# Transposing keys and queries by the DMA crossbar, as 16-bit halves, in a top-k attention with a feed-forward behind it

## Chip, cores and metric

The kernel runs on one core of a Trainium2 chip, in one launch. The metric is device time in microseconds: 1582.88 us is the median of three runs (1582.7 to 1584.52). The profile that is quoted below is one execution with a span of 1580.1 us.

A core has five engines that run side by side, each working through its own instructions strictly in order: TensorE (PE, matrix products into PSUM, with its weight loads shown as PEld), VectorE (DVE), ScalarE (ACT), GpSimd (POOL) and SyncE (SP, whose queue here issues every DMA).[...] An engine whose next instruction has to wait also holds up everything behind it in its own order.

## What is computed

Attention over 8 batches of 8 heads, 576 positions and a head dimension of 64, where each query keeps only the 32 largest of its 576 scores, and then a feed-forward of 512 to 2048 to 512 with a hard-swish between, over all 4608 rows:

```python
scores = scale * np.matmul(q, k.transpose(0, 1, 3, 2))
kth = np.partition(scores, -top_k, axis=-1)[..., -top_k:-top_k + 1]
scores = np.where(scores >= kth, scores, -1e9)
attn = softmax(scores)                     # written out in the reference
x = (attn @ v) -> (B*S, H*D)
h = x @ w_in
out = (h * np.clip(h + 3, 0, 6) / 6) @ w_out
```

Everything is float32.

## The kernel before

**Pairs and duos.** Heads are taken two at a time: a `Pair` is two heads of one batch, four pairs to a batch. Its keys and queries come in as `landed` (128 partitions, nine blocks of 128 columns), and have to be transposed, so that the head dimension lies on the partitions, before TensorE can multiply them. A `Duo` is two pairs and one tile of queries, 128 rows of each of four heads; the 64 rows left over (576 = 4 x 128 + 64) make a smaller "rest" duo. Ten duos make a batch, eight full ones and two rest ones, so there are 80. The rest duos are the last two of batches 0 to 2, duos 2 and 7 of batches 3 to 6, and duos 2 and 3 of batch 7.

**The clock of the program.** The order is written out by hand (`manual_schedule`). The main loop (L562) runs over duos `m` and over eight slots `i`. In each slot VectorE does one round of the top-k search (`top`, L250 and L254: the eight largest of each row, then take them out, four rounds for each of the duo's two halves `u`). Everything else is hung on slots: the table `usual` says how many slots after its duo's start each part of a duo is issued. For half 0: `shift0` at 3, `exp0` at 4, `inverse0` at 9, `weights0` at 10, `flip0` at 12, `join0` at 15; for half 1: `shift1` 7, `exp1` 8, `inverse1` 13, `weights1` 14, `flip1` 16, `join1` 19; then `values` at 22 and `place` at 23. A slot counts as passed with the program's order, not with time, so in a rest duo, whose top-k rounds are about half as long, all the other engines get the same work in some 11 us instead of 19.4.

**A duo's way.** `scores` (PE L227 and L230, then ScalarE copies L233 and L236, in a rest duo L215 to L220) is issued in slot 1 for the next duo. `shift` runs on GpSimd (L263, L266), `exp` on ScalarE (L273, L278, with the row sums `den`, L283), `inverse` on VectorE (L287, the reciprocal of `den`), `weights` on GpSimd (L297, then L306, which splits the 32-bit weights into low and high 16-bit halves `e16`), `flip` is a DMA transpose `t16<-e16` on SP's queue (L312), `join` puts the halves together again (L318, on ScalarE for half 0, on GpSimd for half 1), and `values` multiplies by the values on PE (L338). So the weights are already transposed by the DMA crossbar, as 16-bit halves; the keys and queries are not.

**Feed-forward.** As soon as 128 rows of attention output are placed, a block of feed-forward is queued; `piece` issues it bit by bit between the slots, at a rate that `due` works out from how much is queued: h on PE (L365), evacuations on ScalarE (L373, L375), gates on GpSimd (L379, L380), the second product on PE (L385), the result on ScalarE (L395) and out by DMA (L397).

**Keys and queries.** Of the next batch, pair `p` is loaded in slot 0 of that batch's predecessor's duo 4+p (`pair_at(m, 4)`), by six DMAs, and transposed in slot 5 of duo 5+p (`pair_at(m, 5)`): `Pair.transpose` runs nine TensorE transposes into the one large PSUM tile `big` (L177), and ScalarE copies them out (L179, L180, and L183 twice, the last 64 keys of each head into `kr`). `big` has one buffer, which `scores` uses too.

**Buffers.** `kqpool` has 13 buffers of one size, which `landed`, `kq` (the transposed keys and queries), `e16`, `t16`, `eT` and, at the start, the weights `st` take in turn. In the first four duos the two feed-forward weight matrices are also converted, in 32 chunks, with work on ScalarE, GpSimd and VectorE (L102 to L123).

Of the kernel before, what the change touches and what calls it, by code (L numbers as in the profile page):

```python
# [10 lines left out]
F32 = mybir.dt.float32  # L11
U32 = mybir.dt.uint32
I32 = mybir.dt.int32
U16 = mybir.dt.uint16
# [15 lines left out]
def kernel(  # L30
# [9 lines left out]
    nc = tc.nc  # L40
    P = nc.NUM_PARTITIONS
    B, H, S, D = q.shape
    DM, FF = moe_w_in.shape
    J = S // P
    JP = J * P
    R = S - JP
# [6 lines left out]
    def pool(name, bufs, **kw):  # L53
        return ctx.enter_context(tc.tile_pool(name=name, bufs=bufs, **kw))

    consts = pool("consts", 1)
    kqpool = pool("kq", 13)
    scpool = pool("sc", 3)
    wkpool = pool("wk", 1)
    mpool = pool("m", 4)  # L60
# [27 lines left out]
    def big():  # L88

        return ps_big.tile([P, 5 * 512], F32, tag="big", name="big")  # L90
# [48 lines left out]
    class Pair:  # L139
# [31 lines left out]
        def transpose(self):  # L171
            kq = kqpool.tile([P, JP + S], F32, tag="kq", name="kq")
            self.kT, self.qT = kq[:, 0:JP], kq[:, JP : JP + S]
            ps = big()
            for j in range(2 * J + 1):
                rows = self.landed[:, j, :, :].rearrange("p h d -> p (h d)")
                nc.tensor.transpose(ps[:, j * P : (j + 1) * P], rows, ident[:])  # L177
            c0 = 2 * JP
            nc.scalar.copy(kq[:, 0:c0], ps[:, 0:c0])  # L179
            nc.scalar.copy(kq[:, c0 : c0 + R], ps[:, c0 + R : c0 + 2 * R])  # L180
            for hh in range(2):
                d = slice(hh * D, (hh + 1) * D)
                nc.scalar.copy(self.kr[d, hh, :], ps[d, c0 : c0 + R])  # L183

    class Duo:

# [122 lines left out]
        def flip(self, u):  # L309
            t16 = self.t16[u] = kqpool.tile([P, 2 * (2 * J + 1), P], U16, tag="kq", name="t16")  # L310
            n = 2 * self.nb
            nc.sync.dma_start_transpose(t16[:, 0:n, :], self.e16[u][:, 0 : n * P])  # L312

        def join(self, u):

            eT = self.eT[u] = kqpool.tile([P, 2 * J + 1, P], F32, tag="kq", name="eT")
            copy = nc.gpsimd.tensor_copy if u and not self.early else nc.scalar.copy
            copy(  # L318
                eT[:, 0 : self.nb, :]
                .rearrange("p c q -> p (c q)")  # L320
                .bitcast(U16)
                .rearrange("p (x h) -> p h x", h=2),
                self.t16[u][:, 0 : 2 * self.nb, :].rearrange("p (h c) q -> p h (c q)", h=2),
            )
# [80 lines left out]
    for b in range(B):  # L405
        halves = [pairs[b][0:2], pairs[b][2:4]]
# [18 lines left out]
    def piece(count=1):  # L425
        nonlocal left
        for _ in range(count):
            while todo:
                try:
                    gates.append(next(todo[0]))  # L430
                    left -= 1
                    break
                except StopIteration:
                    todo.pop(0)
            else:
                gates.append(None)
            if len(gates) > 2:
                gate = gates.pop(0)
                if gate:
                    gate()  # L440
# [52 lines left out]
    def convert_step():  # L493


        for c in adding:
            next(c, None)
        adding.clear()
        if len(converting) >= 2 or not landing:
            for c in converting[:1]:  # L500
                next(c)
            adding.extend(converting[:1])
            del converting[:1]
        if landing:
            c = landing.pop(0)
            next(c)
            converting.append(c)
        land()

    def pair_at(m, first):  # L510

        b, at = divmod(m, per_batch)
        return pairs[b + 1][at - first] if b + 1 < B and 0 <= at - first < NHP else None
# [35 lines left out]
    def parts(slot, late=None):  # L549

        for m, part in sorted(queued.get(slot, []), key=lambda x: x[1][:-1] != "shift"):
            if late is not None and (part[:-1] in ("inverse", "weights")) != late:
                continue
            if part == "values":
                values(m)
            elif part == "place":
                place(m)
            else:
                getattr(duos[m], part[:-1])(int(part[-1]))

    due = 0.0
    for m in range(ND + 3):  # L562
        u = duos[m] if m < ND else None
        for i in range(8):
            if u:
                u.top(i // 4, i % 4)
            if m < 4:
                parts(8 * m + i, False)
            convert_step()
            if m == 0 and i == 0:  # L570
                first[3].load()
            if m == 0 and i in (1, 2):
                first[i + 1].transpose()
            if i == (4 if m == 0 else 1) and m + 1 < ND:
                duos[m + 1].scores()
            if m < 4:
                parts(8 * m + i, True)
            else:
                parts(8 * m + i)
            if m == 0 and i in (1, 4):  # L580
                for p in duos[i // 4].pairs:
                    p.load_values()
            if i == 0:
                p = pair_at(m, 4)
                if p:
                    p.load()
            if i == 3 and u and u.pairs[0].b and 1 <= m % per_batch <= 2:
                for p in duos[m - 1].pairs:
                    p.load_values()
            if i == 5:  # L590
                p = pair_at(m, 5)
                if p:
                    p.transpose()

            due += ((left > 0) + (left >= 24) / 8 + (left >= 48) / 8) / (2 if u and u.rest else 1)
            piece(int(due))
            due -= int(due)
# [36 lines left out]
```

## Time and profile before

| | |
|---|---|
| time | 1582.88 us (1582.7 to 1584.52) |
| span of the profiled execution | 1580.1 us, mean granted TensorE clock 0.967 |
| TensorE busy, weight loads busy | 1468.0 us (93%), 1031.7 us (65%) |
| VectorE busy | 1467.4 us (93%) |
| ScalarE busy, GpSimd busy | 1092.8 us (69%), 1144.0 us (72%) |
| TensorE transposes of keys and queries (L177) | 288 instructions, 42.1 us busy |
| ScalarE copies of them out of PSUM (L179, L180, L183) | 32.4, 7.1 and 13.4 us busy |
| GpSimd splits of a full half duo (L306, 128x2304) | 128 of 2104 ns |
| DMA transposes (L312) | 160, 4.6 us from issue to landing (median) |

Two engines stand at 93%, so the table alone doesn't say which of them sets the time. A busy time says how long an engine had an instruction in it; whether another engine could have let it go faster is read from its idle stretches and from what ended them.

### The profile page before, as it was taken

How to read it: one execution, taken by the hardware profiler on the slowest of the kernel's cores; microseconds unless marked ns; L12 is line 12 of the kernel's file. 1: busy time of each engine (PE TensorE's matmuls, PEld its weight loads, DVE VectorE, ACT ScalarE, POOL GpSimd, SP SyncE). 2: the span in 40 equal slices, each digit the busy share in tenths (PEclk: the TensorE clock that was granted, in tenths of full speed). 3: DMA queues.
4: the chain of work that ended last, by engine and by line, in shares of the span. 5: the costliest groups of instructions: out<-in, count | busy, mean ns of one | idle time of the engine just before them, and what ended most of it. 6: DMA issues, size and time to landing. Idle time of an engine off the chain costs nothing.

```text
span 1580.1 us, 28785 instructions
## 1 busy us (share of the span) xinstructions
PE 1468.0 (93%) x10272; PEld 1031.7 (65%) x10272; DVE 1467.4 (93%) x3105; ACT 1092.8 (69%) x1865; POOL 1144.0 (72%) x1264
## 2 busy tenths in 40 slices
PE   5256799799999999999999999999999999999899
PEld 3152666477766776766676776777767776767665
DVE  6999999999999999999999999999999999899800
ACT  6675777677777777678776777778767777777521
POOL 4868687777877787777787777877687777867741
PEclk9667899999999999999999999999999999999999
DMA  8552544444454444455353444445353543533410
GB/s 236 161 180 44 114 83 87 88 91 97 73 101 83 98 83 83 87 97 108 62 108 73 98 88 84 91 93 112 57 110 75 97 88 82 98 62 68 82 23 14
DMA packets 450319, 144.49 MB, mean 91 GB/s; under 512 B 433280, under 2 KB 441472, under 8 KB 450176
## 3 DMA queue, kind: packets, MB, share of 16 engines
q1 hardware_dynamic: 450176, 142.65, 44.0%
q8 instruction: 81, 1.33, 0.3%
q14 instruction: 62, 0.51, 0.1%
HBM read 45.09 MB, written 9.44 MB: 35 GB/s over the span
## 4 chain that ended last, share of the span: by engine, by line
PE 61%; DVE 27%; POOL 4%; issue 3%; ACT 3%; DMA 1%; SPq 1%; POOLq 0%; ACTq 0%; DVEq 0%
PE acc L385 23%; PE h L365 22%; DVE m L250 14%; DVE wk L254 11%; PE pv L338 7%; PE big L227 5%; PE big L230 2%; PE big L177 1%; PE big L215 1%; POOL eT L318 1%; DVE y L118 1%; POOL e L306 1%; DMA t<-e 1%; DVE a L117 1%; POOL sc L297 1%
## 5 line engine op out<-in xcount | busy, mean ns | idle before, releaser
L250 DVE MAX8 m<-wk 128x8 f32<-128x576 f32 x864 | 613.1, 746 | 2.2
L385 PE MATMUL acc<-w_out,g 128*128 128x512 f32 x1152 | 524.1, 603 | 13.5 <-POOL g L380 13.5
L365 PE MATMUL h<-xT,w_in 128*128 128x128 f32 x4096 | 485.2, 278 | 2.8 <-ACT xT L348 2.8
L365 PEld LDWEIGHTS h<-xT,w_in 128*128 128x128 f32 x4096 | 472.6, 194 | 17.0 <-issue 11.6
L254 DVE MATCH_REPLACE8 wk<-m,wk 128x576 f32<-128x576 f32 x576 | 423.7, 742 | 0.0
L385 PEld LDWEIGHTS acc<-w_out,g 128*128 128x128 f32 x1152 | 212.7, 192 | 249.0 <-issue 228.8
L297 POOL TENSOR_SCALAR sc<-sc,den 128x576 f32<-128x576 f32 x288 | 214.1, 754 | 198.1 <-DVE den L287 190.9
L306 POOL COPY e<-sc 128x2304 uint16<-128x2304 uint16 (+1 forms) x192 | 320.4, 1679 | 10.2
L278 ACT ACTIVATE sc<-sc,shift 128x576 f32<-128x576 f32 x288 | 220.5, 771 | 30.2 <-POOL shift L266 27.3
L338 PE MATMUL pv<-eT,vm 128*64 128x128 f32 (+1 forms) x2560 | 164.8, 273 | 68.8 <-ACT eT L318 46.7
L318 ACT COPY eT<-t 128x2304 uint16<-128x2304 uint16 (+1 forms) x82 | 215.9, 2633 | 9.0 <-DMA t<-e 8.9
L273 ACT ACTIVATE sc<-sc,m 128x576 f32<-128x576 f32 x288 | 210.3, 779 | 10.2 <-DVE m L250 9.9
L254 DVE MATCH_REPLACE8 wk<-m,sc 128x576 f32<-128x576 f32 x288 | 211.8, 742 | 0.0
L318 POOL COPY eT<-t 128x2304 uint16<-128x2304 uint16 (+1 forms) x78 | 204.0, 2616 | 8.4 <-DMA t<-e 8.3
L250 DVE MAX8 m<-sc 128x8 f32<-128x576 f32 x288 | 203.3, 743 | 2.9 <-ACT sc L236 2.2
L338 PEld LDWEIGHTS pv<-eT,vm 128*64 128x64 f32 x2560 | 135.4, 141 | 106.1 <-ACT eT L318 48.1
L373 ACT ACTIVATE g<-h,three 128x512 f32<-128x512 f32 x144 | 98.4, 683 | 144.3 <-PE h L365 134.7
L380 POOL TENSOR_TENSOR g<-g,hs 128x512 f32<-128x512 f32 x144 | 184.9, 1284 | 12.0
L379 POOL TENSOR_SCALAR g<-g 128x512 f32<-128x512 f32 x144 | 89.3, 620 | 101.1 <-ACT g L373 92.3
L233 ACT COPY sc<-big 128x2048 f32<-128x2048 f32 (+1 forms) x65 | 119.6, 1839 | 36.7 <-PE big L230 36.2
L227 PE MATMUL big<-kq 64*128 64x512 f32 x512 | 133.6, 641 | 8.2 <-ACT kr L183 5.5
L395 ACT ACTIVATE o<-acc 128x512 f32<-128x512 f32 x36 | 21.4, 594 | 112.1 <-PE acc L385 112.1
(47 smaller groups left out, 1116.6 us busy)
## 6 DMA issues: line engine op xcount, KB each, us to landing
landed<-in_k_dram SPq DMA_DIRECT2D x64, 128.0 KB, 2.9
landed<-in_q_dram SPq DMA_DIRECT2D x64, 128.0 KB, 2.9
st<-in_moe_w_in_dram SPq DMA_DIRECT2D x16, 512.0 KB, 5.0
vm<-in_v_dram SPq DMA_DIRECT2D x64, 128.0 KB, 2.3
st<-in_moe_w_out_dram SPq DMA_DIRECT2D x16, 512.0 KB, 5.5
out_dram<-o SPq DMA_DIRECT2D x32, 256.0 KB, 2.4
t<-e SPq DMA_TRANSPOSE x160, 4.6
landed<-in_k_dram SPq DMA_DIRECT2D x32, 32.0 KB, 2.5
```

The lines of the kernel that those rows point to most:

```text
L227: nc.tensor.matmul(banks[:, 2 * i + hh, :], pr.qT[d, qs], pr.kT[d, :])
L250: nc.vector.max(self.m[u][:, t, 8 * r : 8 * r + 8], self.cur[t])
L254: nc.vector.match_replace(wk, self.m[u][:, t, 8 * r : 8 * r + 8], self.cur[t], LOWEST)
L273: nc.scalar.activation(row, row, AF.Prelu, bias=m[:, t, TOP_K - 1 : TOP_K], scale=-1.0, alpha=FLAT)
L278: nc.scalar.activation(row, row, AF.Exp, bias=self.less[u][:, t : t + 1], scale=-scale / FLAT, accum_out=self.den[:, u, t : t + 1],)
L297: nc.gpsimd.tensor_scalar(row, row, self.den[:, u, t : t + 1], 1.0, ALU.mult, ALU.mult)
L306: nc.gpsimd.tensor_copy(halves[:, :, to : to + c1 - c0], words)
L318: copy(eT[:, 0 : self.nb, :] .rearrange("p c q -> p (c q)") .bitcast(U16) .rearrange("p (x h) -> p h x", h=2), self.t16[u][:, 0 : 2 * self ...
L338: nc.tensor.matmul(pv[hh * D : (hh + 1) * D, u * w : (u + 1) * w], pr.vm[:, hh, c, :] if c < J else pr.vr[:, hh, :], rhs, start=(c == 0), ...
L365: nc.tensor.matmul(h[:, (f - f0) * P : (f - f0 + 1) * P], w_in[:, i, f * P : (f + 1) * P], xT[:, i, :], start=(i == 0), stop=(i == NHP - 1),)
L380: nc.gpsimd.tensor_tensor(g[:], g[:], hs[:], ALU.mult)
L385: nc.tensor.matmul(acc[:], gs[f // nf][:, f % nf * P : (f % nf + 1) * P], w_out[:, f, :], start=(f == 0), stop=(f == NFC - 1),)
```

## The change

For all batches but the first, the nine TensorE transposes of a pair and the copies out of PSUM are replaced by the way that the attention weights already go. GpSimd splits `landed` into 16-bit halves (`split`), one DMA transpose turns them (`flip`), and ScalarE joins them into `kq` and `kr` (`join`, four copies). The load comes one duo earlier, `split` is put in slot 2 and `flip` in slot 5 of duo 4+p, and `join` in slot 1 of duo 5+p. `kqpool` gets a fourteenth buffer, as a pair now needs an `e16` and a `t16` on its way. The aim is to take transposes off TensorE, and PSUM's `big` with them. The first batch's four pairs keep `transpose`.

```diff
-    kqpool = pool("kq", 13)
+    kqpool = pool("kq", 14)
...
+        def split(self):
+            self.e16 = kqpool.tile([P, 2 * (2 * J + 1) * P], U16, tag="kq", name="e16")
+            nc.gpsimd.tensor_copy(
+                self.e16[:].rearrange("p (h x) -> p h x", h=2),
+                self.landed[:]
+                .rearrange("p j h d -> p (j h d)")
+                .bitcast(U16)
+                .rearrange("p (x h) -> p h x", h=2),
+            )
+
+        def flip(self):
+            self.t16 = kqpool.tile([P, 2 * (2 * J + 1), P], U16, tag="kq", name="t16")
+            nc.sync.dma_start_transpose(self.t16[:], self.e16[:])
+
+        def join(self):
+            kq = kqpool.tile([P, JP + S], F32, tag="kq", name="kq")
+            self.kT, self.qT = kq[:, 0:JP], kq[:, JP : JP + S]
+            halves = self.t16[:].rearrange("p (h c) q -> p h (c q)", h=2)
+            def copy(dst, src):
+                nc.scalar.copy(dst.bitcast(U16).rearrange("p (x h) -> p h x", h=2), src)
+            c0 = 2 * JP
+            copy(kq[:, 0:c0], halves[:, :, 0:c0])
+            copy(kq[:, c0 : c0 + R], halves[:, :, c0 + R : c0 + 2 * R])
+            for hh in range(2):
+                d = slice(hh * D, (hh + 1) * D)
+                copy(self.kr[d, hh, :], halves[d, :, c0 : c0 + R])
...
             if i == 0:
-                p = pair_at(m, 4)
+                p = pair_at(m, 3)
                 if p:
                     p.load()
...
-            if i == 5:
-                p = pair_at(m, 5)
+            for at, first_at, part in ((2, 4, "split"), (5, 4, "flip"), (1, 5, "join")):
+                p = pair_at(m, first_at) if i == at else None
                 if p:
-                    p.transpose()
+                    getattr(p, part)()
```

## The prediction

> **What bounds the kernel.** I read the page's busy times, the chain of waits, the waits of VectorE, the windows, then VectorE's timeline at each gap.
>
> ```profile
> PE 1468.0 (93%) x10272; PEld 1031.7 (65%) x10272; DVE 1467.4 (93%) x3105; ACT 1092.8 (69%) x1865; POOL 1144.0 (72%) x1264
> PE 61%; DVE 27%; POOL 4%; issue 3%; ACT 3%; DMA 1%; SPq 1%; POOLq 0%; ACTq 0%; DVEq 0%
> ```
>
> PE and DVE are both at 93%, and the chain puts 61% on PE. That would make 28 pairs of transposes worth having. The windows (columns PE, PEld, DVE, ACT, POOL, clock, DMA share, GB/s) correct this:
>
> ```profile
> 900.00:1000.00 100.00, 100.00 (x700) 68.39 (x700) 99.48 (x215) 72.90 (x127) 76.58 (x85) 1.00 0.43 78
> 1300.00:1400.00 100.00, 100.00 (x697) 66.69 (x697) 95.80 (x205) 71.36 (x119) 76.31 (x88) 1.00 0.39 77
> 1500.00:1540.00 40.00, 39.18 (x234) 26.78 (x235) 0.17 (x1) 11.47 (x19) 18.74 (x19) 0.96 0.10 23
> 1540.00:1580.00 40.00, 36.30 (x180) 23.76 (x178) 0.00 (x0) 5.85 (x10) 7.54 (x8) 1.00 0.04 14
> ```
>
> DVE is busy to the percent all along until it ends its last search at 1494.8, and the last 80 us are feed-forward on PE. In that end, the timeline has PE wait 2.52 us at 1490.4 and 2.47 us at 1500.8 for joined weights, which descend from DVE's last rounds; from 1502.1 it runs a fixed program of 74 us (32 instructions of L385, the last values, two blocks of 128 L365 and 32 L385). So the time is DVE's last search plus a tail that batch 7 fixes, and batch 7 has no pairs to transpose. What PE can give is only what it makes DVE wait:
>
> ```profile
> DVE a L117 <- POOL a L109: 13.3, 2, 10.0
> DVE den L287 <- ACT den L283: 13.3, 5, 8.3
> DVE m L250 <- ACT sc L236: 2.2, 3, 1.5
> ```
>
> (us in total, times, longest.) The first row lies in the first 140 us. Of the second, 8.3 us is the last half duo's, after the searches. DVE's timeline between 160 and 1494.8 us has these gaps:
>
> ```profile
> 587.09 0.17 DVE L287 RECIPROCAL den<-den 128x2 f32<-128x2 f32 x1 [1.06 <-ACT den L283]
> 1182.52 0.17 DVE L287 RECIPROCAL den<-den 128x2 f32<-128x2 f32 x1 [0.71 <-ACT den L283]
> 1374.85 0.16 DVE L287 RECIPROCAL den<-den 128x1 f32<-128x1 f32 x1 [2.82 <-ACT den L283]
> 1378.02 1.42 DVE L250 MAX8 m<-sc 128x8 f32<-128x576 f32 x2 [0.69 <-POOL g L380]
> ```
>
> With 0.47 us at 1274.3, 0.20 at 1006 and 0.11 at 1481, that is **6.06 us: the ceiling of the gain**, 0.38%. All but the last lie in or beside rest duos, where the other engines have some 11 us for a full duo's work.
>
> These gaps come from PE's lag. A duo's scores, due one slot (2.4 us) into the duo before, start on PE 2 to 3 us into it in the early batches, but 6 to 9 us in batches 2 to 6. ScalarE, in order, waits 4.02 us for L365 just ahead of the gap at 587. SP's queue does the same: its first-in-line output DMA waits for PE's result, and the weight flips stand behind it (waits of SP: L397 for L395, 195.2 us). At 1370.2 ScalarE waited 3.05 us for such a flip, and the 2.82 us gap followed.
>
> **What the Trainium skill says.** Perfetto Trace Analysis, Identifying the Most-Contended Engine: TensorE's matmul occupancy "is not a good measure", weight-load share is better. The trace agrees: 93% against 65%. SBUF — State Buffer, Who interferes with whom: a DVE instruction with two SBUF inputs contends with GpSimd's reads, one with a single input doesn't. More GpSimd splits could so slow L250 or L254, but the trace has L254 at 732/742/758 ns (min/median/max) although GpSimd is busy 72% of the time, so I cost it at nothing. DMA: Bandwidth & Descriptors, Rules for kernel authors: issue a DMA early and wait late; transposes of one stream need no mutual wait, and all are on SP here.
>
> **The change part by part** (28 pairs, four for each of seven batches).
>
> *Removed from PE.* Nine transposes occupy PE for 1.15 us together (timeline, L177 x9): 28 x 1.15 = 32 us, and of the 15.0 us idle ahead of them 28/32, some 13 us, mostly waits for `big`. 45 us, 6.5 us a batch: about PE's whole lag. Directly on the end path: 0. Indirectly: up to the 6.06 us.
>
> *Removed from ScalarE.* 1.01 + 0.22 + 2 x 0.21 = 1.66 us a pair (L179, L180, L183).
>
> *Added to ScalarE.* Four copies of 16-bit elements: 2048, 128, 128, 128. ScalarE: Activation LUTs, What ACT_TABLE_LOAD costs, gives 186 ns + 0.833 ns an element: 1.89 + 3 x 0.29 = 2.8 us as an estimate. L318 on ScalarE, the same kind of copy, measures 2.80 us for 2304 and 1.93 for 1536, so 1.13 ns an element and 0.19 us fixed: 2.51 + 3 x 0.34 = 3.5 us. I take 3.5, from the trace. Net +1.9 us a pair, 52 us in all, ScalarE at 69 + 3 = 72 to 73%. Beside other work, except for what is queued behind it: `join` in slot 1 stands ahead of `exp0` in slot 4, so that duo's `den` can be 3.5 us later, where the old copies in slot 5 stood behind `exp0`. Its consumer, DVE's reciprocal, is issued 15.2 us after the search in full duos, with `den` ready after 2.6 to 9 us: hidden. Around rest duos the allowance is 8.7 us (batches 0 to 2, pair 3 joined in duo 8): `den` there came after 3.7, 6.1 and 7.1 us in the three batches; plus 3.5 it would wait 0, 0.9 and 1.9 us at today's lag, nothing at a lag as in batch 0. In batches 3 to 6 pair 2 is joined in the rest duo 7, allowance 11.1, `den` after 3.0 to 7.9: at most 0.3 us.
>
> *Added to GpSimd.* One 128x2304 split, 2104 ns (L306): 28 x 2.1 = 59 us, 72 to 76%. It stands behind `weights0` in the same slot and ahead of `shift0` in slot 3; GpSimd often waits there (190.9 us in total for `den`, L297), and what it delays, `exp0`, is inside the allowance above. In rest duo 7 of batches 3 to 6 it adds up to 2.1 us to the 3.5.
>
> *Added to SP and DMA.* 28 flips of 2.7 us issue and 3.6 to 6.5 us to landing (L312). From slot 5 to slot 1 of the next duo are four slots, 9.7 us. Behind it in the queue: the next flip three slots later, and loads. If SP is late by over 3 to 5 us, ScalarE stands at the join; that needs today's lag of PE (through L397), so it goes with it.
>
> *Load a duo earlier, fourteenth buffer.* 0: loads land in 2.8 us (median) and were used 13 slots later. A pair's own buffers add about one to the count of `kqpool`, and one is added. SP's waits show no load held for long by a buffer now.
>
> *PSUM.* `scores` no longer waits for L183 to leave `big` (12.1 us in all, PE and PEld); counted in PE's lag.
>
> Sum: 6.06 us offered, of which the new work on ScalarE and GpSimd around rest duos takes back about 1. 1582.9 - 4.9 = 1578.0, rounded up for the tail's scatter to **1578.2 us**.
>
> **The rivals.**
> *A, the forecast* (chance 0.53): PE's lag goes, DVE's gaps with it; 1576.8 to 1580.5.
> *B, gain and cost cancel* (0.24): lag shrinks, but joins and splits make `den` as late as PE did: 1582.9. For it: every gap of DVE is at `den` or beside a rest duo, where the new work is put too. Against: `den` has 8 us and more in all other duos.
> *C, slower* (0.23): today's lag stays, for instance as PE's idle time brings the granted clock down (0.63 at 40 to 80 us, where PE is busy 24%), or SP blocks the joins. Waits at the rest duos then come to 2.8 us for `den` of half 0 in batches 0 to 2, some 2 us more for half 1 (allowance 8.7, came after 6.6 to 8.1, plus 1.9), and 2.4 us at the worst rest duo of batches 3 to 6 (7.9 + 3.5 + 2.1 against 11.1): 7.2 us, 1590.
> *D, PE is the bound after all*: 32 to 45 us off, 1538 to 1551. DVE's 1494.8 us less all its idle time, plus the tail, excludes it: under 0.01.
>
> **Numbers.** 1575.5 to 1589 leaves out a little of A's lower end and the upper half of C. Faster by over 0.2% (below 1579.7): most of A and a little of B, 0.50; within: 0.27; slower (above 1586.0): 0.23.
>
> **What would show it.** After: L177 at 36 instructions, PE busy about 1430, ScalarE about 1145, GpSimd about 1200, DVE still 1467; DVE's last search 4 to 5 us sooner, its tail unchanged at 85 us; scores starting 2 to 4 us into the duo in batches 2 to 6; SP's wait L397 for L395 shorter. I am wrong if DVE's waits for `den` grow past 13.3 us, if ScalarE waits for the new flip more than 1 us each time, if L250 gets slower, or if the tail moves.

## The result and the profile after

The changed kernel takes 1589.38 us (median of 4 runs, 1588.47 to 1590.83) against 1583.58 us of the kernel before on the same chip: a ratio of 1.0037, 95% interval 1.002 to 1.0055. It is slower, by 5.8 us, where 4.7 us less were forecast. The profiled execution has a span of 1587.0 us, against 1580.1.

The page of the changed kernel: busy times, then the shares of the chain that ended last.

```profile
PE 1447.4 (91%) x10020; PEld 1008.1 (64%) x10020; DVE 1467.0 (92%) x3105; ACT 1141.9 (72%) x1865; POOL 1199.3 (76%) x1292
PE 55%; DVE 19%; POOL 14%; ACT 5%; issue 4%; DMA 2%; SPq 1%; POOLq 0%; ACTq 0%
```

VectorE has the same work to within 0.4 us. TensorE has 20.6 us less, ScalarE 49 and GpSimd 55 us more. GpSimd's share of the chain has gone from 4% to 14%. That is a hint of where to look and no more: two of the faster versions below have 12% and 19%.

The new operations, from the groups by line with shapes kept apart (count, then busy us and mean ns, then idle us before them):

```profile
L206 ACT COPY kq<-t 128x2048 uint16<-128x2048 uint16 x28 | 70.8, 2530 | 0.0
L188 POOL COPY e<-landed 128x2304 uint16<-128x2304 uint16 x28 | 59.1, 2110 | 0.0
L206 ACT COPY kr<-t 64x128 uint16<-64x128 uint16 x56 | 18.8, 336 | 0.3
L206 ACT COPY kq<-t 128x128 uint16<-128x128 uint16 x28 | 9.7, 345 | 0.0
L177 PE MATMUL big<-ident,landed 128*128 128x128 f32 x36 | 9.0, 427 | 9.9 <-DMA landed<-in_k_dram 6.6 <-ACT sc L266 2.5 <-DMA landed<-in_q_dram 0.7
```

Every one costs what was worked out for it, and ScalarE has all but no idle time ahead of the joins (0.3 us): the flips land in time. So the loss isn't in the price of an operation. VectorE's waits, answering to those shown of before:

```profile
DVE den L317 <- ACT den L313: 18.7, 8, 8.4
DVE a L117 <- POOL a L109: 13.9, 2, 10.6
DVE m L280 <- ACT sc L266: 1.7, 2, 1.0
DVE m L280 <- POOL eT L348: 1.4, 1, 1.4
```

And VectorE's timeline at the gaps between 160 us and its last search:

```profile
415.63 0.16 DVE L317 RECIPROCAL den<-den 128x1 f32<-128x1 f32 x1 [1.06 <-ACT den L313]
601.09 0.16 DVE L317 RECIPROCAL den<-den 128x1 f32<-128x1 f32 x1 [1.92 <-ACT den L313]
604.96 1.42 DVE L280 MAX8 m<-sc 128x8 f32<-128x576 f32 x2 [1.40 <-POOL eT L348]
1188.74 0.17 DVE L317 RECIPROCAL den<-den 128x2 f32<-128x2 f32 x1 [3.09 <-ACT den L313]
1380.70 0.16 DVE L317 RECIPROCAL den<-den 128x1 f32<-128x1 f32 x1 [3.04 <-ACT den L313]
1383.86 1.42 DVE L280 MAX8 m<-sc 128x8 f32<-128x576 f32 x2 [0.69 <-ACT sc L266]
```

With three of 0.1 to 0.2 us these come to 11.7 us, where before there were 6.1. That is 5.6 us more, nearly all in or next to rest duos, and it is the loss: VectorE's last search ends at 1500.6 us in place of 1494.8. No gap is named after the new operations. The reciprocal waits for `den` of ScalarE, as it did before. What made `den` late has to be found behind it.

One number points to it. Over the 28 duos that carry a split, `shift0` (GpSimd, L293 and L296) ends on average 1.7 us after its search before the change and 3.8 us after it, and `den` of that half comes 4.9 and 7.3 us after the search. The step of the shift is 2.1 us, one split. That of `den` is 2.4 us and has two parts: by the same mean it is 5.9 us in the version below that leaves out the split and 6.2 us in the kernel before with nothing but a split, so the longer join on ScalarE adds about 1 us and the split 1.3. GpSimd's timeline in one of these duos (duo 27, which starts at 559.7 us on VectorE) shows the order:

```profile
565.48 1.48 POOL L327 TENSOR_SCALAR sc<-sc,den 128x576 f32<-128x576 f32 x2 [4.48 <-DVE den L317]
567.02 2.10 POOL L336 COPY e<-sc 128x2304 uint16<-128x2304 uint16 x1
569.07 2.11 POOL L188 COPY e<-landed 128x2304 uint16<-128x2304 uint16 x1
571.27 0.61 POOL L409 TENSOR_SCALAR g<-g 128x512 f32<-128x512 f32 x1
571.96 1.28 POOL L410 TENSOR_TENSOR g<-g,hs 128x512 f32<-128x512 f32 x1
573.20 0.20 POOL L293 TENSOR_TENSOR shift<-m 128x2 f32<-128x2 f32 x1
573.49 0.22 POOL L296 TENSOR_SCALAR shift<-shift 128x2 f32<-128x2 f32 x1
573.65 2.81 POOL L348 COPY eT<-t 128x2304 uint16<-128x2304 uint16 x1
```

GpSimd idles 4.48 us until the reciprocal lets it weight the rows (L327). Then it works without a pause: split of the weights, split of keys and queries (L188), a gate, the shift, the join of the weights of an earlier half (L348). Two lines of the kernel before, in the same duo, which began at 557.8 us there:

```profile
563.56 1.47 POOL L297 TENSOR_SCALAR sc<-sc,den 128x576 f32<-128x576 f32 x2 [4.98 <-DVE den L287]
569.67 2.82 POOL L318 COPY eT<-t 128x2304 uint16<-128x2304 uint16 x1
```

The new split has been put *behind* the wait, near the head of the busy stretch, so all that follows in it is 2.1 us later: the join starts 13.95 us into the duo, and before it started 11.87 us into it.

### The profile page after: what moved, and what is told of

Same layout as the page of the kernel before. It is cut to its first block, busy times and chain, and to the rows that moved or that the text cites. A ratio compares the mean times of both kernels' runs of the same rounds, so it can differ in the third digit from the quotient of the medians.

```text
span 1587.0 us, 28285 instructions
## 1 busy us (share of the span) xinstructions
PE 1447.4 (91%) x10020; PEld 1008.1 (64%) x10020; DVE 1467.0 (92%) x3105; ACT 1141.9 (72%) x1865; POOL 1199.3 (76%) x1292
## 4 chain that ended last, share of the span: by engine, by line
PE 55%; DVE 19%; POOL 14%; ACT 5%; issue 4%; DMA 2%; SPq 1%; POOLq 0%; ACTq 0%
PE acc L415 22%; PE h L395 19%; DVE m L280 10%; DVE wk L284 8%; PE pv L368 7%; PE big L257 4%; POOL eT L348 2%; POOL e L336 2%; POOL sc L327 2%; POOL g L410 2%; PE big L260 2%; POOL a L109 1%; ACT sc L308 1%; ACT eT L348 1%; POOL e L188 1%
## 5 line engine op out<-in xcount | busy, mean ns | idle before, releaser
L327 POOL TENSOR_SCALAR sc<-sc,den 128x576 f32<-128x576 f32 x288 | 213.7, 753 | 155.6 <-DVE den L317 155.0
L368 PE MATMUL pv<-eT,vm 128*64 128x128 f32 (+1 forms) x2560 | 168.7, 278 | 97.5 <-POOL eT L348 52.5
L348 ACT COPY eT<-t 128x2304 uint16<-128x2304 uint16 (+1 forms) x82 | 215.9, 2633 | 9.9 <-DMA t<-e 9.8
L348 POOL COPY eT<-t 128x2304 uint16<-128x2304 uint16 (+1 forms) x78 | 203.4, 2608 | 13.0 <-DMA t<-e 12.9
```

Of the source, the lines that this page charges most:

```text
L327: nc.gpsimd.tensor_scalar(row, row, self.den[:, u, t : t + 1], 1.0, ALU.mult, ALU.mult)
L348: copy(eT[:, 0 : self.nb, :] .rearrange("p c q -> p (c q)") .bitcast(U16) .rearrange("p (x h) -> p h x", h=2), self.t16[u][:, 0 : 2 * self ...
L368: nc.tensor.matmul(pv[hh * D : (hh + 1) * D, u * w : (u + 1) * w], pr.vm[:, hh, c, :] if c < J else pr.vr[:, hh, :], rhs, start=(c == 0), ...
```

## The experiments

Theory S: the split, by its place in GpSimd's order, holds up the shift, the gate and the weights' join behind it; what follows from them on ScalarE and TensorE eats the gain. Rival J: ScalarE's longer join stands ahead of `exp0`. Rival F: the flip, in SP's queue or on the DMA engines. A later rival, W: GpSimd's total work is what counts, wherever it is put. In the tables, "gaps" is VectorE's idle time between 160 us and its last search, gaps over 0.1 us, and "lag" is how far into the duo before a duo's scores start on TensorE, mean of batches 2 to 6; both from the timelines.

### One part taken away at a time

The split left out for all pairs but one:

```diff
-    kqpool = pool("kq", 14)
+    kqpool = pool("kq", 13)
...
+    once = consts.tile([P, 2 * (2 * J + 1) * P], U16, tag="once", name="once")
...
-            self.e16 = kqpool.tile([P, 2 * (2 * J + 1) * P], U16, tag="kq", name="e16")
+            self.e16 = once
+            if (self.b, self.hp) != (1, 0):
+                return
             nc.gpsimd.tensor_copy(
```

> The changed kernel, but GpSimd's split is done for one pair only, into a constant tile, and the 27 other pairs flip and join that tile (so they use the wrong keys and queries[...]). It leaves out 27 x 2.1 us of GpSimd; flip, join, loads and a pair's place in the order stay, and the pool has 13 buffers as a pair's e16 is gone. Theory S (the split stands ahead of the weights' join on GpSimd, TensorE then waits for it at the values, and gives back what it gained): VectorE's idle time between 160 us and its last search falls from 11.7 us to 6 or less, TensorE's waits for GpSimd's eT from 52 us to under 30, time 1577 to 1582, ratio to before 0.996 to 0.999. Rival J (ScalarE's longer join ahead of exp): no change from the changed kernel, ratio 1.003 to 1.005. Rival F (the flip in SP's queue and on the DMA engines): the same, 1.003 to 1.005.

The join made cheap:

```diff
-            copy(kq[:, 0:c0], halves[:, :, 0:c0])
...
+            words = self.t16[:, 2 * J + 1 :, :].rearrange("p c q -> p (c q)").bitcast(F32)
+            for at in (0, JP):
+                nc.scalar.copy(kq[:, at : at + JP], words[:, 0:JP])
...
```

> The changed kernel, but ScalarE's join of keys and queries copies 32-bit words of the high halves alone, in five plain copies of 512, 512, 64, 64 and 64 elements (about 1.9 us a pair in place of 3.5, near the 1.7 us of the old copies); what they hold are not the keys and queries. Theory S: little change, ratio 1.002 to 1.005. Rival J: ScalarE's den comes 1.6 us sooner beside the joins, ratio 0.997 to 1.000. Rival F: 1.003 to 1.005.

The flip left out:

```diff
-            self.t16 = kqpool.tile([P, 2 * (2 * J + 1), P], U16, tag="kq", name="t16")
-            nc.sync.dma_start_transpose(self.t16[:], self.e16[:])
+            pass
...
-            halves = self.t16[:].rearrange("p (h c) q -> p h (c q)", h=2)
+            halves = self.e16[:].rearrange("p (h x) -> p h x", h=2)
```

> The changed kernel without the DMA transposes of keys and queries: the join reads the split halves untransposed, so scores are of wrong numbers; split and join stay, 28 transposes of 160 + 28 are left out and so is their t16. Theory S: little change, ratio 1.002 to 1.005. Rival J: the same. Rival F: the loss goes, 0.997 to 1.000, and SP's waits for the split (85 us in the changed kernel) with it.

And the split alone, added to the kernel before (its `split` is that of the change, into a tile that nobody reads):

```diff
-    kqpool = pool("kq", 13)
+    kqpool = pool("kq", 14)
...
-                p = pair_at(m, 4)
+                p = pair_at(m, 3)
...
+            if i == 2:
+                p = pair_at(m, 4)
+                if p:
+                    p.split()
```

> The kernel before with TensorE's transposes and ScalarE's copies kept, and to it only the load a duo earlier, the fourteenth buffer and GpSimd's split in slot 2, whose result nobody reads. Theory S: slower than before, by as much as the change or more, since TensorE is not relieved: ratio 1.003 to 1.008. Rivals J and F: no change, 0.999 to 1.001.

| kernel | time us | ratio to before (interval) | gaps us | lag us |
|---|---|---|---|---|
| before | 1583.22 | 1 | 6.1 | 5.7 |
| the change | 1589.38 | 1.0037 (1.002 to 1.0055) | 11.7 | 6.0 |
| no split | 1578.95 | 0.9972 (0.9962 to 0.9983) | 2.5 | 4.2 |
| cheap join | 1587.48 | 1.0027 (1.0017 to 1.0037) | 10.7 | 6.0 |
| no flip | 1589.74 | 1.0039 (1.0025 to 1.0053) | 13.0 | 6.2 |
| before, with a split | 1591.89 | 1.0053 (1.0041 to 1.0066) | 14.3 | 6.7 |

(The time of before is that of the runs these four share; the change was measured beside its own, 1583.58.) The split decides it. Without it the change is 4.3 us faster than before; with nothing but it, before is 8.7 us slower. The flip costs nothing that can be told from the scatter: leaving out 28 transposes gives 1.0039 (1.0025 to 1.0053) against 1.0037. (SP's waits that end at a split's flip come to 65 us in the changed kernel, not 85 as put there.) The cheap join is worth 1 us in VectorE's gaps, and its ratio's interval overlaps that of the change, so J is at most a minor part. The three kernels that join wrong words give VectorE the same work: it is busy for 1466.6 to 1467.1 us in them. VectorE's waits for `den` say the same as the times, first of the kernel without the split, then of the kernel before with it:

```profile
DVE den L320 <- ACT den L316: 10.1, 3, 8.6
```

```profile
DVE den L297 <- ACT den L293: 22.1, 10, 10.3
```

8.6 and 10.3 us of these are the one wait after the last search, which is in every version (8.3 us before). The rest is 1.5 us against 11.8, where it was 5.0 before and 10.3 in the change.

One mark was missed. TensorE's waits for GpSimd's `eT` (L348) were expected to fall below 30 us without the split and stood at 46.5, against 52.5 in the change and 22.0 before. They are not where the loss is, as they are nearly as long in this fast version. The likely reading is that a TensorE with less to do reaches the joined weights sooner and waits for them longer; the kernel before with a split, where it isn't relieved, has 27.6 us.

### Where the split stands

If the order is what hurts, the split can be moved. Ahead of `weights0`, into the wait that the timeline above shows:

```diff
-            for at, first_at, part in ((2, 4, "split"), (5, 4, "flip"), (1, 5, "join")):
+            for at, first_at, part in ((1, 4, "split"), (5, 4, "flip"), (1, 5, "join")):
```

> The changed kernel with the split one slot sooner, in slot 1, so ahead of weights0 on GpSimd instead of behind it; all else the same. Theory S, in its form for the order on GpSimd (the split delays shift0 and join1, which come after it): GpSimd has idle time ahead of weights0 (155 us in all in the changed kernel, waiting for the reciprocal), so where that is over 2.1 us the split costs nothing: shift0 1.5 to 3 us after its search in place of 3.8, VectorE's idle between 160 us and its last search 3 to 8 us in place of 11.7, ratio to before 0.997 to 1.001. Rival W (GpSimd's total work is what counts, 1198 us however placed): ratio 1.003 to 1.005 as in the changed kernel.

Or behind the shift and the join:

```diff
+            for at, first_at, part in ((3, 4, "split"), (6, 4, "flip"), (1, 5, "join")):
```

> The changed kernel with the split in slot 3, behind shift0 and join1 on GpSimd, and the flip in slot 6. Theory S in its form for the order: shift0 and join1 are not delayed, weights1 in slot 6 is at most by some 2 us, which has slack: ratio 0.997 to 1.001, shift0 about 1.7 us after its search. Rival W: 1.003 to 1.005.

The split in slot 1, and the join on ScalarE moved behind `exp0`:

```diff
+            for at, first_at, part in ((1, 4, "split"), (5, 4, "flip"), (5, 5, "join")):
```

> The split in slot 1 and besides the join in slot 5, behind exp0 on ScalarE, where the old copies stood. Theory S alone: as the split in slot 1 alone. If the join ahead of exp0 costs too (the cheap join gave 1.6 us or nothing): 1 to 3 us less than the split in slot 1 alone, 0.996 to 0.999. Rival W: 1.003 to 1.005.

All of it in one duo:

```diff
+            for at, first_at, part in ((0, 4, "split"), (2, 4, "flip"), (5, 4, "join")):
```

> Split in slot 0, flip in slot 2 and join in slot 5 of the same duo 4+p, a duo sooner than in the change for the join, behind exp0. The split is ahead of everything of its duo on GpSimd save the shift of slot 7 before it; the join has 3 slots (7.3 us) for the flip, which needs 4.6 us to landing. Theory S: 0.996 to 1.001 if the flip lands in time; if it doesn't, ScalarE stands at the join (a wait on the DMA at the join's line over 20 us in all) and it is slower, 1.002 to 1.006. Rival W: 1.003 to 1.005.

| kernel | time us | ratio to before (interval) | gaps us | lag us | shift0, den us after the search |
|---|---|---|---|---|---|
| before | 1582.96 | 1 | 6.1 | 5.7 | 1.7, 4.9 |
| the change (slot 2) | 1589.38 | 1.0037 (1.002 to 1.0055) | 11.7 | 6.0 | 3.8, 7.3 |
| split in slot 1 | 1579.01 | 0.9972 (0.9961 to 0.9984) | 3.2 | 5.0 | 2.3, 6.3 |
| split in slot 3 | 1580.5 | 0.9987 (0.998 to 0.9993) | 4.5 | 4.9 | 2.0, 6.4 |
| slot 1, join in slot 5 | 1579.3 | 0.9976 (0.9967 to 0.9985) | 3.3 | 4.9 | 2.3, 4.8 |
| slots 0, 2, 5 of one duo | 1579.64 | 0.9975 (0.9965 to 0.9985) | 2.7 | 5.0 | 2.3, 4.9 |

(Last column: half 0 of the 28 duos with a split; a mean over each.) One digit in the slot table turns the loss into a gain. Moving the split from slot 2 to slot 1 is worth 10 us, with the same instructions: GpSimd is busy 1199.4 us in it and 1199.3 us in the change. W is out. And the split in slot 1 is as fast as no split at all (0.9972 both), so there it costs nothing that can be measured. GpSimd's timeline in the same duo, which begins at 557.4 us here, shows why:

```profile
558.13 2.10 POOL L188 COPY e<-landed 128x2304 uint16<-128x2304 uint16 x1
563.16 1.47 POOL L327 TENSOR_SCALAR sc<-sc,den 128x576 f32<-128x576 f32 x2 [2.93 <-DVE den L317]
564.69 2.10 POOL L336 COPY e<-sc 128x2304 uint16<-128x2304 uint16 x1
566.88 0.61 POOL L409 TENSOR_SCALAR g<-g 128x512 f32<-128x512 f32 x1
567.58 1.28 POOL L410 TENSOR_TENSOR g<-g,hs 128x512 f32<-128x512 f32 x1
568.81 0.20 POOL L293 TENSOR_TENSOR shift<-m 128x2 f32<-128x2 f32 x1
569.11 0.22 POOL L296 TENSOR_SCALAR shift<-shift 128x2 f32<-128x2 f32 x1
569.27 2.82 POOL L348 COPY eT<-t 128x2304 uint16<-128x2304 uint16 x1
```

The split now lies ahead of the wait; the wait is still there, 2.93 us long in place of 4.98 before the change, and in this duo everything behind it is where it was, the join at 11.87 us into the duo. (Over the 28 duos the shift is still 0.5 us later, 2.3 against 1.7 us.) The join's place on ScalarE moves `den` by 1.5 us (6.3 to 4.8) and the time by nothing that can be told from the scatter, so `den` had that much to spare with the shift on time. In the one-duo version the flip lands within its three slots in all but two of the 28 joins, for which ScalarE waits 3.8 us in all.

Slot 3 shows that what counts is which instructions are held up. There the split stands behind the wait as well, in the same busy stretch, but behind the shift and the join:

```profile
563.22 1.47 POOL L327 TENSOR_SCALAR sc<-sc,den 128x576 f32<-128x576 f32 x2 [4.57 <-DVE den L317]
569.33 2.83 POOL L348 COPY eT<-t 128x2304 uint16<-128x2304 uint16 x1
572.05 2.13 POOL L188 COPY e<-landed 128x2304 uint16<-128x2304 uint16 x1
576.22 1.48 POOL L327 TENSOR_SCALAR sc<-sc,den 128x576 f32<-128x576 f32 x2
```

The join is at 11.9 us into the duo, and it is the weights of half 1 (the last line, at 574.12 us with the split in slot 1) that the split holds up. That costs 1.5 us against slot 1, with intervals that overlap a little, and not 10.

### Controls

The load a duo earlier and the fourteenth buffer alone, on the kernel before:

```diff
-    kqpool = pool("kq", 13)
+    kqpool = pool("kq", 14)
...
-                p = pair_at(m, 4)
+                p = pair_at(m, 3)
```

> The kernel before with nothing but the load a duo earlier and the fourteenth buffer: the control for the two runs that add a split to the kernel before. Theory S: nothing, ratio 0.999 to 1.001. If load or buffer had a part in the loss of the changed kernel: 1.002 or more.

The same with the idle split, in slot 1:

```diff
+            if i == 1:
+                p = pair_at(m, 4)
+                if p:
+                    p.split()
```

> The kernel before with the early load, the fourteenth buffer and the idle split as in the earlier run, but in slot 1, ahead of weights0. Theory S in its form for the order: most of the 8 us that the split in slot 2 cost is gone, ratio 0.999 to 1.003. Rival W (GpSimd's total): 1.004 to 1.007 as in slot 2.

The version with the split in slot 1, on 13 buffers:

```diff
-    kqpool = pool("kq", 14)
+    kqpool = pool("kq", 13)
```

> The split in slot 1 with 13 buffers in place of 14. If the buffer count is as tight as the count by slots says (peak 12 of 14): 0.1 to 0.3% slower than the same with 14, 0.998 to 1.001 against before; if the peak is not reached in time: the same, 0.996 to 0.998.

| kernel | time us | ratio to before (interval) | gaps us |
|---|---|---|---|
| before | 1583.34 | 1 | 6.1 |
| early load, 14 buffers | 1582.83 | 0.9999 (0.9991 to 1.0007) | 5.8 |
| the same with a split in slot 1 | 1583.28 | 1.0000 (0.9992 to 1.0008) | 6.3 |
| split in slot 1, 13 buffers | 1583.28 | 1.0005 (0.9997 to 1.0013) | 4.7 |

Load and buffer by themselves do nothing, so the 8.7 us that the split in slot 2 cost the kernel before are the split's, and moving it by one slot removes them all. The fourteenth buffer is needed once there is a gain to lose: with 13 the gain of the slot-1 version is gone, though the forecast for it was open. The trace doesn't explain all of it: the gaps in it are only 1.4 us longer, where the medians are 4.3 us apart, and it is of the fastest of the 13 executions (1581.03 us; the slowest took 1586.81). What holds up the slower ones is open.

## Why the prediction was wrong

**Right: what bounds the kernel.** VectorE's searches and a tail set the time, TensorE's 93% notwithstanding. The change in gaps (5.6 us) gives the change in time (5.8), and across the versions the time follows the gaps: the time less the gaps is 1575.8 to 1577.7 us in all of them but the one with 13 buffers (1578.6). The ceiling of 6.1 us holds as well: the best versions gain 3.3 to 4.3 us and leave 2.5 to 3.3 us of gaps.

**Right in size, wrong in its parts: the value of TensorE's relief.** "6.06 us offered, of which the new work takes back about 1" made 1578.2 us. Without the split, or with it in slot 1, the runs show 1579.0. But the relief was booked too high. The transposes did lose what was put down for them (L177 from 42.1 to 9.0 us), while TensorE's busy time in all fell by 20.6 us and not by 32, and the idle time ahead of L177 from 15.0 to 9.9 us and not by 13. The waits of `scores` for L183, booked under PSUM, didn't go at all. First before, then after the change:

```profile
PEld big L227 <- ACT kr L183: 6.7, 3, 2.7
PE big L227 <- ACT kr L183: 5.5, 3, 2.3
```

```profile
PEld big L257 <- ACT kr L183: 6.8, 3, 3.0
PE big L257 <- ACT kr L183: 5.6, 3, 2.6
```

None of them comes after the first 160 us: they belong to the first batch, whose pairs keep `transpose`. The lag, too, was read too high: "6 to 9 us in batches 2 to 6" is 5.7 us in the mean, and it falls to 4.2 and 5.0 us in these two versions, not to the "2 to 4" that the forecast needed. So that the gain came out nearly as forecast is in part luck: the gaps shrank to 2.5 and 3.2 us with most of the lag still there.

**Right: the prices.** Join 3.5 us (2.53 + 0.35 + 2 x 0.34), split 2.1 us, flip 2.8 us of issue and 4.9 to landing (medians of the 28), and no search slowed by GpSimd's added work (VectorE's busy time 1467.0 against 1467.4 us).

**Wrong: the step on GpSimd.** The prediction had the order right, "behind `weights0` in the same slot and ahead of `shift0`", and then costed it at nothing beyond the rest duos: "GpSimd often waits there (190.9 us in total for `den`, L297), and what it delays, `exp0`, is inside the allowance". The first half is the error. The 190.9 us are waits *before* L297, and the split was issued *after* it, where the timeline of duo 27 has no idle time left. The idle total was read without asking on which side of it the new work lands. The second half fails with it: the allowance of 15.2 us was right for a full duo, but the delay doesn't end with the duo. The shift, the gate and the join each come 2.1 us later there, and the gaps turn up elsewhere: the one that grew most, from 0.71 to 3.09 us (at 1182.5 us before, 1188.7 after), is in duo 62, a rest duo that comes five duos after the last one with a split. How the delay travels that far was not followed step by step.

**Wrong: "PE's lag goes".** The sum let the relief of TensorE cancel the delays, and set the two side by side as if independent. With the split in slot 2 the lag is 6.0 us, no less than before. GpSimd's lateness can reach TensorE through the weights' join and the gates, both behind the split in order. That it is the split that keeps the lag up is shown by the runs (6.7 with it alone, 4.2 without); which of join, gate and shift carries how much of it is open, as no run held up one of them alone. Slot 3 says only that it is these three together, and not the work of half 1 behind them, that make most of the loss.

**The rival that came true** is C in its direction and almost its number (1590), but not in its causes. SP didn't block the joins. The granted clock fell from 0.967 to 0.959 in the mean, but it doesn't go with the time: the split in slot 1 has 0.962 and gains, the kernel before with a split has 0.964 and loses. C was right that the lag stays, without a reason for it. Its near hit is in part luck, as the waits are not where its sum has them: it has 2.8 us for `den` of half 0 in batches 0 to 2, where 1.1 were measured, and 2.4 us at the rest duo 7 of a batch from 3 to 6, where there is no gap at all, while the 3.09 us of duo 62 are in no term of it.

**The marks.** Met: L177 at 36, ScalarE and GpSimd within 4 us, VectorE's work unchanged. Missed: TensorE 1447 and not 1430 us, the last search 5.8 us later and not 4 to 5 sooner, SP's wait for the output at 190.4 and not well below 195.2 us, the scores 6.0 us into the duo and not 2 to 4. And a sign that it had named for being wrong came: VectorE's waits for `den` grew past 13.3 us, to 18.7. The tail moved from 85.3 to 86.4 us, but it is 85.5 to 86.7 in all the other runs, 86.2 in the control with before's own tail, so a microsecond there is scatter.

**A version that beats both.** The change with `split` in slot 1 takes 1579.01 us, 0.9972 of the kernel before (0.9961 to 0.9984).

## What to carry to other kernels

When work is added to an engine that takes its instructions in order, the engine's idle time hides it if the work stands ahead of the wait that makes the idle time; behind it, the same instruction delays what follows up to the next wait. So find the engine's idle stretch in the timeline, read off which instruction ends it, and place the new work in front of that instruction. Where that isn't possible, place it behind the instructions whose results are needed soonest: in slot 3 the split cost little, though it stands behind the wait. And relief for one engine doesn't pay while another engine's lateness feeds back into it: cost the two together, not side by side.

## What the runs showed that was not expected

Some 28 instructions of 2.1 us, on an engine that is idle a quarter of the time, moved the time by 10 us through one slot of order (1589.38 against 1579.01 us). The single fourteenth buffer turned out to be worth 0.3% in the slot-1 version (1.0005 against 0.9972), while on the kernel before it was worth nothing. And TensorE's waits for GpSimd's joined weights more than doubled in the fastest version too (22.0 us before, 46.0 us with the split in slot 1): the growth of a wait named after an engine is no sign that the engine costs time.
